# The last pair's attention weights scaled on VectorE, and gate/value products of 256 more tokens placed in the attention stage

## The chip, the cores and the metric

The kernel runs on one core of one Trainium2 chip. A core has five engines with a queue of instructions each: PE (TensorE, matrix products; PEld are its weight loads), DVE (VectorE), ACT (ScalarE), POOL (GpSimd) and SP (SyncE, which here only issues DMAs). The metric is the device time of one execution in microseconds. Three timed runs of the kernel before took 1032.08, 1032.63 and 1033.08 us; the median is 1032.63 us. The profiled execution, from which all rows below come, took 1029.82 us, of which 1028.0 us are the span from the first to the last instruction.

## The reference

Attention with a compressive memory over 4 batches, 8 heads, 576 tokens and 64 dimensions, then two gated feed-forward layers over all 2304 tokens:

```
scores = q k^T / 8, causal;  a = softmax(scores);  local = a v
phi(x) = elu(x) + 1;  mem_out = (phi(q) M_prev) / (phi(q) z_prev + 1e-6)
attn   = g * mem_out + (1 - g) * local          with g = sigmoid(beta) per head
x      = attn as 2304 tokens x 512
x      = (silu(x w_gate) * (x w_val)) w_out     w_gate, w_val: 512 x 1536, w_out: 1536 x 512
out    = act(x w_in) w_out2                     w_in: 512 x 2048, w_out2: 2048 x 512
act(h) = h if h >= 1; 0 if h <= -1; (h + 1)^2 / 4 between
```

The feed-forward weights are drawn in float64 and the activations in float32, and the kernel keeps some 22 bits: each operand of a large product is split into a high and a low part of a shorter type, and each product is done as three (high x low, low x high, high x high).

## The kernel before, in words

The kernel has two parts, each a list of tasks that a small planner (`Plan`) puts in order when the program is built. A task has an engine, an estimated duration, a priority, tasks it depends on and buffers it uses (`Inst`). The planner plays the tasks through with its estimates, each engine taking the ready task of best priority, and the instructions are emitted in the order that comes out. On the chip each engine then works through its own list in order, and waits at an instruction until what it needs is done. The estimates themselves are in no instruction.

*The attention stage* (`Attention.pair`, 0 to about 254 us) has 16 groups of tasks, one for each batch and pair of heads, called pairs here. For a pair, PE transposes keys and queries, forms the scores (`s`, L643 and L677), DVE takes the row minimum of the negated, masked scores (L657, L684), ACT forms the exponentials and their sums (L664, L695), DVE inverts the sums (`scales`, L719 and L723), and nine instructions multiply the weights `a` by that inverse and by 1 - g (`scale`, L732). These nine run on POOL. PE then transposes the scaled weights (`t`, L743, L745, L766, L783), ACT and DVE copy the transposes out of PSUM into `R` (L446), and PE forms the output with the values (`av`, L808 and L815), which ACT and DVE split into two parts and SP stores to `xs` in DRAM (L844). For phi(q), POOL folds and normalizes `p` (L581, L591). The planner gives the eight PSUM banks out one at a time, so a product waits for the copy that empties its bank.

Attention leaves PE with spare time, so part of the first feed-forward layer stands in it. `early_x` loads tokens of `xs` back into four `xh` tiles (L1144), and `early_unit` forms the gate or value product of a block of 128 columns of the weights (an f block) for these tokens: 12 products on PE (L1166), a copy by ACT into one of three `gvo` buffers (L1172) and a store to `gv` in DRAM (L1176). This is done for f blocks 0 to 5, which are three pairs of f blocks, and tokens 0 to 511. The planner is given the same tasks once more for the next two groups of tokens, as ghosts: they take time and buffers in the plan, and emit nothing.

*The second part* begins with a plain stage (`plain`, L1353, about 254 to 372 us): the rest of f blocks 0 to 5. Its tokens come in six groups of 384 (`HB`), two to a `kb`. For group 1, tokens 384 to 767, tokens 384 to 511 come from `gv` (`from_gv`: loads at L1373, silu at L1378, multiplication at L1379) and the other 256 are formed by products. Each call of `plain` fills two of eight PSUM banks, which ACT (silu, L1360) and DVE (multiplication, L1361) empty. The inputs `xw` are quarters of a group, loaded at L1275: four by POOL's queue at the end of its list, the others by SP's. Then come the f blocks 6 to 11 in a scheme with seven products in place of eight (`chain`, L1402), whose weights DVE and ACT split beforehand (L893 to L951), the product with w_out (L1480), and the second layer (L1402 again, and L1534). Order on PE is fixed there; the other engines follow by due times.

Of the kernel before, what the change touches and what calls it, by code (L numbers as in the profile page):

```python
# [18 lines left out]
P = 128  # L19
# [7 lines left out]
D0 = 6  # L27
# [13 lines left out]
HB = NT // NG  # L41
HS = S // 2
HT = 512
SET_AHEAD, PARK_AHEAD, H_AHEAD, H2_AHEAD, W_AHEAD, W2_AHEAD = 40000, 60000, 20000, 20000, 12000, 7000
MASKED = -8.0e9

# [255 lines left out]
def c_pool(n):  # L302
    return 0.835 * n + 285
# [23 lines left out]
class Attention:  # L327
# [81 lines left out]
    def pair(self, b, n):  # L409
# [15 lines left out]
        def add(eng, dur, name, fn, deps=(), uses=(), port=False, form=0):  # L425
            t = pl.add(eng, dur, at_of(name), fn, deps, uses, port=port, form=form)
            t["name"] = name
            return t
# [299 lines left out]
        def scale(key, h, i, cols, name, t_r):  # L728
            def f():
                a = st["a"][key][:, 0:cols]  # L730
                o = i if h == 0 else i + 5
                nc.gpsimd.tensor_scalar(a, a, st["mn"]["r"][:, o:o + 1], self.OGP[:, n, o:o + 1], op0=ALU.mult, op1=ALU.mult)  # L732
            return add("POOL", c_pool(cols), name + ".sc", f, [t_r], [i_a[key], i_mn])

        def tr4(t_r):
            t = scale(4, 0, 0, S, "t4", t_r)
# [354 lines left out]
def tile_attention_two_moe(  # L1091
# [11 lines left out]
    half = cst.tile([P, 1], F32, name="half")  # L1103
    nc.gpsimd.memset(half, 0.5)
    xs = dram.tile([P, KT, 2, NT], F32, name="xs")
    gv = [[dram.tile([P, 2, HT], F32, name=f"gv{i}_{j}") for j in range(2)] for i in range(D0 // 2)]
    hs = [[dram.tile([P, 2, HB], F32, name=f"hs{i}_{g}") for g in range(NG)] for i in range(F1 // 2)]
    h2s = [[dram.tile([P, 2, HB], F32, name=f"h2s{i}_{g}") for g in range(NG)] for i in range(F2 // 2)]
    wts = Weights(ctx, tc, dram)
# [5 lines left out]
    with ExitStack() as actx:  # L1115
        warm = actx.enter_context(tc.tile_pool(name="warm", bufs=1))
        plan = Plan({"PE": 4500, "POOL": 8500, "DVE": 4800}, over={"PE": 15, "ACT": 40, "DVE": 40, "POOL": 50}, lat={"DMA": 1500},
                    slow={"PE": (15500, 1.7)}, stay=STAY, turn=TURN)
        wts.pooled = True
        wts.begin(actx, plan, {"raw": 2, "wA": 3, "wS": 1}, "a", "pool")  # L1120
        still = warm.tile([P, P], F32, name="still")
        nc.vector.memset(still, 0.0)
        at = Attention(actx, tc, plan, q, k, v, M_prev, z_prev, beta, {"ident": ident}, xs)
        fpool = actx.enter_context(tc.tile_pool(name="fp", bufs=1))
        gpool = actx.enter_context(tc.tile_pool(name="gp", bufs=1))
        plan.cap("gvo", GVO), plan.cap("xh", XH)
        idle = at.ps.tile([P, HT], F32, name="idle", tag="bank7")
        for _ in range(WARM):
            nc.tensor.matmul(idle[:, 0:P], still, still, start=True, stop=True)
        for n, ((kind, f), prio) in enumerate(zip(first, EARLY)):  # L1130
            units[kind, f] = wts.early(plan, in_cols(moe_w_gate if kind == "gate" else moe_w_val, f), prio,
                                       trios[n // 3], n % 3)

        def early_x(tok, prio, deps, ghost, last):


            s, n = {"x": [None] * KT, "i": [], "t": []}, tok.stop - tok.start
            for kt in range(KT):
                i_x = plan.inst("xh")

                def f(kt=kt, i_x=i_x):
                    if not ghost:
                        s["x"][kt] = fpool.tile([P, 2, n], F32R, name="xh", tag=f"xh{i_x.slot}")
                        nc.sync.dma_start(f32(s["x"][kt]), xs[:, kt, :, tok])  # L1144

                s["i"].append(i_x)
                s["t"].append(plan.dma(prio, [n * 2.85], f, deps[kt], [i_x], last))
                last = plan.last
            return s, last

        def early_unit(f, x, prio, own, ghost):


            s = {}
            for j, kind in enumerate(("gate", "val")):
                u = units[kind, f]
                i_p, i_o = plan.inst("bank"), plan.inst("gvo")

                def prod(i, u=u, j=j, i_p=i_p):
                    if ghost:  # L1160
                        return
                    if i == 0:
                        s[j] = at.ps.tile([P, HT], F32, name="mm", tag=f"bank{i_p.slot}")
                    for kt in range(CUTS[i], CUTS[i + 1]):
                        for n, (pw, px) in enumerate(PARTS):
                            nc.tensor.matmul(s[j], u["k"](pw, kt), x["x"][kt][:, px], start=(kt == 0 and n == 0),  # L1166
                                             stop=(kt == KT - 1 and n == 2))

                def copy(j=j, i_o=i_o):
                    if not ghost:  # L1170
                        s["o", j] = gpool.tile([P, HT], F32, name="gvo", tag=f"gvo{i_o.slot}")
                        nc.scalar.copy(s["o", j], s[j])  # L1172

                def put(j=j):
                    if not ghost:
                        nc.sync.dma_start(gv[f // 2][j][:, f % 2], s["o", j])  # L1176

                t = []
                for i in range(len(CUTS) - 1):
                    cost = 3 * (CUTS[i + 1] - CUTS[i]) * (HT + 32) / 2.4  # L1180
                    t = [plan.add("PE", cost, prio - (i > 0), lambda i=i, prod=prod: prod(i),
                                  t + [*u["t"], *x["t"][CUTS[i]:CUTS[i + 1]]],
                                  [i_p, *x["i"][CUTS[i]:CUTS[i + 1]]])]
                t = plan.add("ACT", c_act(HT), prio - 1, copy, t, [i_p, i_o])
                if own:
                    t = plan.add("ACT", 50, prio - 2, put, [t], [i_o])
                    plan.add("DMA", 1.42 * HT, prio, lambda: None, [t], [i_o])
                else:
                    plan.dma(prio, [1.42 * HT], put, [t], [i_o])

        t_x, last = {}, None
        for b in range(B):
            t_x[b] = [at.pair(b, n) for n in range(NP)]
            if b < B - 1:
                tok, ghost = slice(b * HT, (b + 1) * HT), b > 0
                stored = [[t_x[e][kt] for e in range(tok.start // S, b + 1)] for kt in range(KT)]
                xh, last = early_x(tok, X_AT[b], stored, ghost, last)
                for f in range(D0):
                    early_unit(f, xh, GROUP_AT[b], b == B - 2 and f >= D0 - 2, ghost)
        with tc.manual_schedule():  # L1200
            plan.emit()

# [362 lines left out]


    for i in range(D0 // 2):
        t = flat("h")
        kept = [from_gv(i, HT - HB, HB, t, 15000)]
        ends = kept + [plain(f, qs[0], 1, slice(HT - HB, HB), t, []) for f in (2 * i, 2 * i + 1)]  # L1570
        t_hs[i, 1] = store(t, hs[i][1], ends)
    for r in range(2):
        qs[0][r, 0] = quarter(0, r, 0, 8000)
# [105 lines left out]
```

## Time and profile before

| | |
|---|---|
| median of three timed runs | 1032.63 us |
| profiled execution | 1029.82 us |
| its span | 1028.0 us |
| busy: PE, PEld, DVE, ACT, POOL | 98%, 88%, 69%, 56%, 21% |
| chain that ended last, by engine | PE 94%, POOL 3%, DMA 1%, DVE 1%, issue 1% |
| mean granted PE clock | 0.994 of full speed |

A group of the profile is one line of the kernel on one engine, written with what it writes and reads (`mm<-xw`). PE's matrix products overlap, so the time per product is the busy time of a group divided by its count, and not the mean duration of one. The busy share of PE is nearly full everywhere but for one of the forty slices of the page, the one from about 231 to 257 us, where it is 6 tenths. [...]

### The profile page before, as it was taken

The page shows a single profiled execution, that of the slowest core. Times are in us where ns is not written, and L with a number is a line of the kernel's source. Part 1 is how long each engine was busy: PE and PEld are TensorE (multiplying, and loading weights), DVE is VectorE, ACT ScalarE, POOL GpSimd, SP SyncE. Part 2 cuts the span into 40 slices and gives each one's busy share as a digit, 9 for nine tenths or more (in the row PEclk, how much of TensorE's full clock was granted, in tenths as well). Part 3 has the DMA queues.
Part 4 walks back from the last instruction along what each step waited for, and adds up shares of the span by engine and source line. Part 5 has one row for each costly group of instructions (what it writes and reads, how often), then busy time and mean ns, then how long its engine had stood idle before and what let it go on. Part 6 is the DMA issues. An engine that isn't in the chain of part 4 may idle for free.

```text
span 1028.0 us, 16598 instructions
## 1 busy us (share of the span) xinstructions
PE 1004.1 (98%) x5892; PEld 907.8 (88%) x5892; DVE 705.9 (69%) x1483; ACT 576.5 (56%) x1247; POOL 219.9 (21%) x309
## 2 busy tenths in 40 slices
PE   6999999996999999999999999999999999999998
PEld 5667777775999999999999999999999988888886
DVE  5888888874697777777858988866765346455451
ACT  5987898864333254536344444454444558566561
POOL 7899889994000000000000000000000000000000
PEclk9999999998999999999999999999999999999999
DMA  7786654324975551524986575145443596324320
GB/s 173 179 228 192 170 166 132 107 90 167 353 263 183 181 172 59 164 99 154 376 319 230 179 252 195 52 159 184 159 164 134 193 369 231 120 79 150 129 102 31
DMA packets 142883, 180.93 MB, mean 176 GB/s; under 512 B 70160, under 2 KB 99856, under 8 KB 142800
## 3 DMA queue, kind: packets, MB, share of 16 engines
q1 hardware_dynamic: 140702, 176.42, 52.0%
q0 software_dynamic: 768, 3.15, 0.9%
q8 instruction: 47, 0.77, 0.3%
q10 hardware_dynamic: 1330, 0.30, 0.1%
q14 instruction: 36, 0.29, 0.1%
HBM read 114.82 MB, written 65.01 MB: 175 GB/s over the span
## 4 chain that ended last, share of the span: by engine, by line
PE 94%; POOL 3%; DMA 1%; DVE 1%; issue 1%; SPq 0%; POOLq 0%; DVEq 0%
PE mm L1402 30%; PE mm L1534 19%; PE mm L1480 15%; PE mm L1353 11%; PE av L815 4%; PE mm L1166 3%; PE s L643 3%; PE t L766 2%; PE av L808 2%; POOL a L732 1%; PE s L677 1%; PE t L783 1%; PE tq L539 1%; PE tp L597 1%; PE tk L528 1%; PE t L743 1%
## 5 line engine op out<-in xcount | busy, mean ns | idle before, releaser
L1402 PE MATMUL mm<-xw 128*128 128x384 f32 x1512 | 269.8, 335 | 0.5 <-DVE xw L951 0.5
L1402 PEld LDWEIGHTS mm<-xw 128*128 128x128 f32 x1512 | 262.7, 188 | 0.9 <-DVE xw L951 0.8
L1534 PE MATMUL mm<-xw 128*128 128x512 f32 x864 | 196.2, 390 | 0.0
L1534 PEld LDWEIGHTS mm<-xw 128*128 128x128 f32 x864 | 162.3, 188 | 33.5
L1480 PE MATMUL mm<-xw 128*128 128x384 f32 x864 | 150.1, 334 | 0.0
L1480 PEld LDWEIGHTS mm<-xw 128*128 128x128 f32 x864 | 149.8, 188 | 0.0
L1353 PE MATMUL mm<-xw 128*128 128x384 f32 (+1 forms) x720 | 117.4, 324 | 0.0
L1353 PEld LDWEIGHTS mm<-xw 128*128 128x128 f32 x720 | 117.1, 189 | 0.2 <-issue 0.2
L732 POOL TENSOR_SCALAR a<-a,r,OGP 128x256 f32<-128x256 f32 (+4 forms) x144 | 96.1, 679 | 4.8 <-ACT a L664 3.2
L664 ACT ACTIVATE a<-a,mn 128x256 f32<-128x256 f32 (+3 forms) x128 | 71.0, 565 | 9.3 <-DVE mn L657 9.1
L1523 DVE SCALAR_TENSOR_TENSOR t<-r,t 128x768 f32<-128x768 f32 x48 | 46.0, 958 | 39.2 <-ACT t L1522 37.6
L1297 DVE TENSOR_TENSOR xw<-t,xw 128x768 fp32r<-128x768 f32 x48 | 46.0, 957 | 37.0 <-ACT xw L1294 37.0
L1294 ACT CAST xw<-t 128x768 fp32r<-128x768 f32 x48 | 40.1, 835 | 40.6 <-DVE t L1523 40.6
L657 DVE CUSTOM_DVE_ANT_0 a<-s,mask 128x512 f32<-128x512 f32 (+3 forms) x128 | 55.1, 485 | 4.9 <-PE s L643 4.5
L888 ACT ACTIVATE wA<-raw 128x512 f32<-128x512 f32 x68 | 45.6, 677 | 21.3 <-DMA raw<-in_moe_w_out_dram 15.7
L1424 ACT COPY mm<-mm 128x384 f32<-128x384 f32 x42 | 19.5, 465 | 57.5 <-PE mm L1402 57.5
L815 PEld LDWEIGHTS av<-R,vn 128*64 128x64 f32 x448 | 32.2, 137 | 21.3
L1402 PE MATMUL mm<-xw,wh 128*128 128x384 f32 x252 | 50.4, 334 | 0.0
L1520 ACT ACTIVATE t<-r,half 128x768 f32<-128x768 f32 x48 | 44.9, 936 | 8.9 <-DMA r<-h2s 8.0
L1294 ACT CAST xw<-h 128x768 fp32r<-128x768 f32 x36 | 29.7, 836 | 34.5 <-DMA h<-hs 21.2
L815 PE MATMUL av<-R,vn 128*64 128x320 f32 (+4 forms) x448 | 48.7, 357 | 0.0
L899 DVE SCALAR_TENSOR_TENSOR wA<-raw,wA 128x512 uint32<-128x512 uint32 x68 | 48.3, 716 | 0.3
(142 smaller groups left out, 1528.8 us busy)
## 6 DMA issues: line engine op xcount, KB each, us to landing
h2s<-r SPq DMA_DIRECT2D x48, 384.0 KB, 2.5
r<-h2s SPq DMA_DIRECT2D x48, 384.0 KB, 3.8
raw<-in_moe_w_out_dram SPq DMA_DIRECT2D x28, 512.0 KB, 6.3
park<-pk SPq DMA_DIRECT2D x28, 512.0 KB, 2.9
hs<-h SPq DMA_DIRECT2D x36, 384.0 KB, 4.7
h<-hs SPq DMA_DIRECT2D x36, 384.0 KB, 5.0
xw<-park SPq DMA_DIRECT2D x24, 512.0 KB, 7.9
xs<-x SPq DMA_DIRECT2D x16, 576.0 KB, 4.3
```

The source lines that it names most:

```text
L657: nc.vector.tensor_tensor_reduce(a, st[f"s{h}{tag}"][:, at_[c]:at_[c] + kl[c]], self.mask0[:, 512 - kl[c]:512], -0.125, 3.0e38, ALU.add, A ...
L664: nc.scalar.activation(a, a, AF.Exp, bias=mn[:, o:o + 1], scale=-1.0, accum_out=sm[:, o, 0:1])
L732: nc.gpsimd.tensor_scalar(a, a, st["mn"]["r"][:, o:o + 1], self.OGP[:, n, o:o + 1], op0=ALU.mult, op1=ALU.mult)
L815: nc.tensor.matmul(o[rg][halves[h], c0:c1], st["vn"][:, kc, h], r, start=False, stop=i == len(terms[rg]) - 1, tile_position=(0, h * 64), s ...
L899: nc.vector.scalar_tensor_tensor(s["F"], words(s["raw"])[:, :, 1], 0xC0000000, s["F"], op0=ALU.bitwise_and, op1=ALU.bitwise_or)
L1294: nc.scalar.copy(s["x"][:, :, 0], t())
L1297: nc.vector.tensor_sub(s["x"][:, :, 1], t(), f32(s["x"][:, :, 0]))
L1353: nc.tensor.matmul(o[:, 0:n], u["k"](pw, kt), qs[kt // 2, c]["at"](px, kt % 2)[:, span], start=(kt == 0 and i == 0), stop=(kt == KT - 1 an ...
L1402: nc.tensor.matmul(o, S["k"](k, pw, j), x[k]["at"](px, j), start=begin and not (i or j), stop=j == 1 and i == 2, skip_group_check=True)
L1480: nc.tensor.matmul(o, u["k"](pw, m), h["at"](px, j), start=(i == 0 and j == 0 and n == 0), stop=(i == F1 // 2 - 1 and j == 1 and n == 2), ...
L1523: x1 = add_dve(2 * HB, lambda raw=raw, t=t: nc.vector.scalar_tensor_tensor(t["get"](), raw["get"](), 1.0, t["get"](), op0=ALU.max, op1=ALU ...
L1534: nc.tensor.matmul(o, h["at"](px, j)[:, m * P:(m + 1) * P], u["w"][:, pw], start=(i == 0 and j == 0 and n == 0), stop=(i == F2 // 2 - 1 an ...
```

## The change

Two things are changed. For the last of the 16 pairs, the nine scales of L732 are issued on DVE, and the planner counts them there; the other fifteen stay on POOL. And the f blocks 0 and 1 get tokens 512 to 767 in the attention stage too (`GV` says up to which token each pair of f blocks is done there): `early_x` now loads these 256 tokens into `xh`, and four units form their products with 256 columns. Their results go to `gv`, and in the plain stage group 1 of these two blocks is read from `gv` whole, 384 columns, without products. For the other blocks, and for the last group of tokens, the tasks stay ghosts; the sizes that the planner is told for ghosts follow the slices of tokens, so they are smaller.

```diff
--- before.py
+++ after.py
@@ -41,6 +41,7 @@
 HB = NT // NG
 HS = S // 2
 HT = 512
+GV = (768, 512, 512)
 SET_AHEAD, PARK_AHEAD, H_AHEAD, H2_AHEAD, W_AHEAD, W2_AHEAD = 40000, 60000, 20000, 20000, 12000, 7000
 MASKED = -8.0e9
 
@@ -729,8 +730,11 @@
             def f():
                 a = st["a"][key][:, 0:cols]
                 o = i if h == 0 else i + 5
-                nc.gpsimd.tensor_scalar(a, a, st["mn"]["r"][:, o:o + 1], self.OGP[:, n, o:o + 1], op0=ALU.mult, op1=ALU.mult)
-            return add("POOL", c_pool(cols), name + ".sc", f, [t_r], [i_a[key], i_mn])
+                eng.tensor_scalar(a, a, st["mn"]["r"][:, o:o + 1], self.OGP[:, n, o:o + 1], op0=ALU.mult, op1=ALU.mult)
+
+            eng = nc.vector if num == B * NP - 1 else nc.gpsimd
+            return add(*(("DVE", c_dve(cols)) if num == B * NP - 1 else ("POOL", c_pool(cols))), name + ".sc", f, [t_r],
+                       [i_a[key], i_mn])
 
         def tr4(t_r):
             t = scale(4, 0, 0, S, "t4", t_r)
@@ -1103,7 +1107,7 @@
     half = cst.tile([P, 1], F32, name="half")
     nc.gpsimd.memset(half, 0.5)
     xs = dram.tile([P, KT, 2, NT], F32, name="xs")
-    gv = [[dram.tile([P, 2, HT], F32, name=f"gv{i}_{j}") for j in range(2)] for i in range(D0 // 2)]
+    gv = [[dram.tile([P, 2, GV[i]], F32, name=f"gv{i}_{j}") for j in range(2)] for i in range(D0 // 2)]
     hs = [[dram.tile([P, 2, HB], F32, name=f"hs{i}_{g}") for g in range(NG)] for i in range(F1 // 2)]
     h2s = [[dram.tile([P, 2, HB], F32, name=f"h2s{i}_{g}") for g in range(NG)] for i in range(F2 // 2)]
     wts = Weights(ctx, tc, dram)
@@ -1148,10 +1152,10 @@
                 last = plan.last
             return s, last
 
-        def early_unit(f, x, prio, own, ghost):
-
-
-            s = {}
+        def early_unit(f, x, tok, prio, own, ghost):
+
+
+            s, size = {}, tok.stop - tok.start
             for j, kind in enumerate(("gate", "val")):
                 u = units[kind, f]
                 i_p, i_o = plan.inst("bank"), plan.inst("gvo")
@@ -1163,17 +1167,17 @@
                         s[j] = at.ps.tile([P, HT], F32, name="mm", tag=f"bank{i_p.slot}")
                     for kt in range(CUTS[i], CUTS[i + 1]):
                         for n, (pw, px) in enumerate(PARTS):
-                            nc.tensor.matmul(s[j], u["k"](pw, kt), x["x"][kt][:, px], start=(kt == 0 and n == 0),
+                            nc.tensor.matmul(s[j][:, 0:size], u["k"](pw, kt), x["x"][kt][:, px], start=(kt == 0 and n == 0),
                                              stop=(kt == KT - 1 and n == 2))
 
                 def copy(j=j, i_o=i_o):
                     if not ghost:
-                        s["o", j] = gpool.tile([P, HT], F32, name="gvo", tag=f"gvo{i_o.slot}")
-                        nc.scalar.copy(s["o", j], s[j])
+                        s["o", j] = gpool.tile([P, size], F32, name="gvo", tag=f"gvo{i_o.slot}")
+                        nc.scalar.copy(s["o", j], s[j][:, 0:size])
 
                 def put(j=j):
                     if not ghost:
-                        nc.sync.dma_start(gv[f // 2][j][:, f % 2], s["o", j])
+                        nc.sync.dma_start(gv[f // 2][j][:, f % 2, tok], s["o", j])
 
                 t = []
                 for i in range(len(CUTS) - 1):
@@ -1192,11 +1196,11 @@
         for b in range(B):
             t_x[b] = [at.pair(b, n) for n in range(NP)]
             if b < B - 1:
-                tok, ghost = slice(b * HT, (b + 1) * HT), b > 0
+                tok = slice(b * HT, min((b + 1) * HT, GV[0]))
                 stored = [[t_x[e][kt] for e in range(tok.start // S, b + 1)] for kt in range(KT)]
-                xh, last = early_x(tok, X_AT[b], stored, ghost, last)
+                xh, last = early_x(tok, X_AT[b], stored, b == 2, last)
                 for f in range(D0):
-                    early_unit(f, xh, GROUP_AT[b], b == B - 2 and f >= D0 - 2, ghost)
+                    early_unit(f, xh, tok, GROUP_AT[b], b == B - 2 and f >= D0 - 2, b * HT >= GV[f // 2])
         with tc.manual_schedule():
             plan.emit()
 
@@ -1565,9 +1569,10 @@
 
 
     for i in range(D0 // 2):
-        t = flat("h")
-        kept = [from_gv(i, HT - HB, HB, t, 15000)]
-        ends = kept + [plain(f, qs[0], 1, slice(HT - HB, HB), t, []) for f in (2 * i, 2 * i + 1)]
+        t, n = flat("h"), GV[i] - HB
+        ends = [from_gv(i, n, HB, t, 15000)]
+        if n < HB:
+            ends += [plain(f, qs[0], 1, slice(n, HB), t, []) for f in (2 * i, 2 * i + 1)]
         t_hs[i, 1] = store(t, hs[i][1], ends)
     for r in range(2):
         qs[0][r, 0] = quarter(0, r, 0, 8000)
```

The two kernels have the same order on every engine up to about 226 us. Three places follow.

On PE, at the end of the attention stage (`t` transposes of weights, `a_3369` and `a_3339` those of the pair before the last, `a_3574` and `a_3552` of the last), before:

```order
L766 MATMUL t_3548<-ident,a_3369 128x128 x3
L766 MATMUL t_3555<-ident,a_3339 128x128 x4
L743 MATMUL t_3563<-ident,a_0_237 128x128 x4
L745 MATMUL t_3568<-ident,a_0_237 128x128
L766 MATMUL t_3610<-ident,a_3574 128x128 x3
L766 MATMUL t_3616<-ident,a_3552 128x128 x3
```

and in the changed kernel, where the lines after 1100 stand four higher, L1170 is L1166 and the last pair's weights are `a_3577` and `a_3560`:

```order
L770 MATMUL t_3556<-ident,a_3369 128x128 x3
L1170 MATMUL mm<-xh,xw 128x256 x48
L770 MATMUL t_3665<-ident,a_3577 128x128 x3
L770 MATMUL t_3671<-ident,a_3560 128x128 x3
L770 MATMUL t_3677<-ident,a_3339 128x128 x4
L770 MATMUL t_3682<-ident,a_3553 128x128 x4
L770 MATMUL t_3688<-ident,a_3543 128x128 x4
```

The 48 products stand behind the first three transposes; four transposes of the pair before the last and that pair's `t` of L743 and L745 now come behind them, the latter as the last but one group ahead of the output's products.

On DVE, from the sums of the last pair on (`r` the inverse sums, `OGP` the factors 1 - g), before:

```order
L719 TENSOR_REDUCE r<-sum_225 128x5
L723 RECIPROCAL r<-r 128x5
L719 TENSOR_REDUCE r<-sum_225 128x4
L723 RECIPROCAL r<-r 128x4
L446 COPY R_3625<-t_3616 128x3x128
```

and in the changed kernel:

```order
L724 RECIPROCAL r<-r 128x5
L733 TENSOR_SCALAR a_3571<-a_3571,r,OGP 128x256
L733 TENSOR_SCALAR a_3573<-a_3573,r,OGP 128x128
L733 TENSOR_SCALAR a_3543<-a_3543,r,OGP 128x512
L733 TENSOR_SCALAR a_3560<-a_3560,r,OGP 128x384
L720 TENSOR_REDUCE r<-sum_225 128x4
L733 TENSOR_SCALAR a_1_238<-a_1_238,r,OGP 128x576
L724 RECIPROCAL r<-r 128x4
L733 TENSOR_SCALAR a_3581<-a_3581,r,OGP 128x256
L733 TENSOR_SCALAR a_3590<-a_3590,r,OGP 128x128
L733 TENSOR_SCALAR a_3553<-a_3553,r,OGP 128x512
L733 TENSOR_SCALAR a_3577<-a_3577,r,OGP 128x384
```

The nine scales stand between the sums and the copies of transposes, four of them ahead of the second head's sum; the copies to `R` follow them, among them one that stood ahead of the sums.

On SP, from the store of the third pair from the end on, before:

```order
L844 DMA xs<-x 128x2x576
L1176 DMA gv_0_70<-gvo 128x512
L844 DMA xs<-x 128x2x576
L1373 DMA h<-gv_0_68 128x2x128
L1373 DMA v<-gv_1_69 128x2x128
L844 DMA xs<-x 128x2x576
```

and in the changed kernel:

```order
L848 DMA xs<-x 128x2x576
L1148 DMA xh<-xs 128x2x256 x3
L1180 DMA gv_0_70<-gvo 128x512
L1148 DMA xh<-xs 128x2x256
L1180 DMA gv_0_68<-gvo 128x256
L1180 DMA gv_1_69<-gvo 128x256
L1180 DMA gv_0_68<-gvo 128x256
L1180 DMA gv_1_69<-gvo 128x256
L848 DMA xs<-x 128x2x576
L1377 DMA h<-gv_0_68 128x2x384
L848 DMA xs<-x 128x2x576
L1377 DMA v<-gv_1_69 128x2x384
```

Four loads of `xh` and four stores of `gv` with 256 columns are new, all ahead of the last two pairs' stores, and the first load of `h` now stands ahead of the last pair's store. On POOL the nine scales are gone from the end of the list, so its four loads of `xw` follow the last pair's product `p` (L591) directly.

## Rows read from the trace of the kernel before

**Rows 1.** chain that ended last, by time: start us, us, what

```profile
240.27 1.19 POOL a L732 x2
...
371.78 86.33 PE mm L1402 x498
...
459.16 0.61 DVE xw L951
```

**Rows 2.** timeline of PE: start us, us, instruction, operands, count [idle before <-releaser]

```profile
232.65 0.98 PE L766 MATMUL t<-ident,a 128*128 128x128 f32 x7
...
242.16 3.05 PE L766 MATMUL t<-ident,a 128*128 128x128 f32 x14 [7.98 <-POOL a L732]
...
246.88 0.76 PE L808 MATMUL av<-P,MZ 128*64 128x320 f32 x4
...
254.39 7.82 PE L1353 MATMUL mm<-xw 128*128 128x256 f32 x63
```

**Rows 3.** timeline of POOL at the end of the attention stage

```profile
236.25 1.15 POOL L591 TENSOR_TENSOR p<-p,nrm 128x576 f32<-128x576 f32 x1 [2.83 <-DVE nrm L587]
237.38 5.52 POOL L732 TENSOR_SCALAR a<-a,r,OGP 128x256 f32<-128x256 f32 x9
242.85 3.20 POOL L1275 DMA_DIRECT2D xw<-xs  x4
```

**Rows 4.** windows: us, busy PE PEld DVE ACT POOL, PEclk, DMA share, GB/s

```profile
231.00:234.00 3.00, 3.00 (x26) 2.29 (x24) 2.54 (x11) 1.81 (x6) 2.26 (x4) 1.00 0.01 3
...
237.00:240.00 3.00, 0.00 (x0) 0.00 (x0) 0.34 (x2) 0.78 (x4) 3.00 (x6) 0.67 0.00 0
...
244.00:245.00 1.00, 1.00 (x7) 1.00 (x6) 0.70 (x2) 0.00 (x0) 1.00 (x2) 0.56 0.73 83
245.00:246.00 1.00, 1.00 (x11) 1.00 (x10) 0.94 (x2) 0.43 (x1) 1.00 (x2) 1.00 0.68 207
```

**Rows 5.** waits from 254 us on: engine line <- releaser: us, times, longest

```profile
PEld mm L1402 <- DVE xw L951: 0.8, 1, 0.8
...
DVE h L1361 <- PE mm L1353: 14.4, 15, 2.5
```

**Rows 6.** groups by line and shape: count, busy us, mean ns, idle

```profile
L893 DVE TENSOR_SCALAR wA<-wA 128x512 f32<-128x512 f32 x56 | 23.6, 422 | 21.0 <-ACT wA L888 20.9
...
L951 DVE TENSOR_TENSOR pk<-wA,pk 128x512 fp32r<-128x512 f32 x28 | 19.2, 686 | 3.5 <-ACT pk L949 3.5
...
L1353 PE MATMUL mm<-xw 128*128 128x256 f32 x144 | 17.5, 284 | 0.0
```

**Rows 7.** timeline of SP, whose instructions issue DMAs

```profile
229.49 0.33 SPq L1176 DMA_DIRECT2D gv<-gvo  x1
...
258.71 1.15 SPq L1275 DMA_DIRECT2D xw<-xs  x2
```

**Rows 8.** DMA issues: tiles, queue, count, KB each, median us to landing

```profile
xw<-xs SPq DMA_DIRECT2D x8, 768.0 KB, 12.2
...
gv<-gvo SPq DMA_DIRECT2D x12, 256.0 KB, 6.6
...
v<-gv SPq DMA_DIRECT2D x3, 128.0 KB, 4.6
```

**Rows 9.** timeline of all engines inside the gap

```profile
234.59 0.85 ACT L446 COPY R<-t 128x256 f32<-128x256 f32 x4
234.75 0.69 DVE L446 COPY R<-t 128x512 f32<-128x512 f32 x1
...
236.55 0.19 DVE L723 RECIPROCAL r<-r 128x5 f32<-128x5 f32 x1
...
237.58 0.20 ACT L664 ACTIVATION_READ_ACCUMULATOR a<-a,mn 128x1 f32 x1
```

**Rows 10.** line 893 up to 250 us: duration ns min/median/max, first and last start

```profile
L893 DVE TENSOR_SCALAR wA<-wA x12: 397/427/873, 9.3 to 208.1; 128x512 f32<-128x512 f32 x12
```

**Rows 11.** timeline of DVE ahead of the stage at L1402

```profile
369.12 0.42 DVE L951 TENSOR_TENSOR xw<-wC,xw 128x256 fp32r<-128x256 f32 x1
```

## The prediction

> **What bounds the kernel now.** I read the page first: PE is busy for 98% of the span and carries 94% of the chain that ended last, so a change pays where PE stands still, or where it leaves PE less to do. The forty slices show one dip, in slice 10, about 231 to 257 us. There the chain in order of time [rows 1] leaves PE for L732 on POOL, and then runs on PE without a break from 371.78 to 458.11 us. The PE timeline [rows 2] shows the dip as one gap: seven transposes at 232.65, then fourteen at 242.16 behind an idle time of 7.98 us, from 234.18 on, that POOL ended. The POOL timeline [rows 3] says what it did meanwhile: the product p of the last pair to 237.40, then nine scales in a row until 242.90. [...] So this place costs 7.98 us of idle time and half of 2.7 us, 1.35: 9.3 us in all. Behind 254.39 PE waits for nothing longer than 0.8 us [rows 5].
>
> **The change, part by part.** *Products that leave the second stage.* 144 products of 256 columns at L1353 took 17.5 us of PE [rows 6], 0.1215 us each. 48 of them go (two f blocks, gate and value, 12 each): 48 x 0.1215 = 5.83 us. They stood in a stretch where PE waits for nobody, so all of it comes off, if what follows is ready 5.83 us earlier (below).
>
> *The same 48 products in the attention stage.* PE issues them behind three of the seven transposes, at 232.65 + 3/7 of 0.82 (to the next line's start) = 233.0, for 5.83 us, to 238.8. That is inside the gap, so their cost is nothing as long as the gap would have been there; what covers them is the wait for the last pair's scaled weights. Nine transposes that stood ahead of the gap (1.2 us) move behind them; they filled PE before and fill it after, so they cancel.
>
> *Their inputs.* Four loads of xh, 256 KB each, stand on SP's queue around the store of 229.49 [rows 7]. The buffers come free as the last 512-column products read them; the last of the four is issued behind that store, at about 229.9. A store of the same 256 KB issued at 229.49 left no more than a share of 0.01 of the DMA engines busy after 231 [rows 4], so under 2 us; by that the last load lands at 232. PE first reads that tile at its 16th product, 233.0 + 15 x 0.12 = 234.8: free. By the other end, 6.6 us, the median of such stores in busier stretches [rows 8], it lands at 236.5 and costs 1.7 us. I take nothing, the quiet store being the nearer row.
>
> *The nine scales, from POOL to DVE.* First, when they can start. DVE had a copy of 0.69 us at 234.75 ahead of the sums, ACT four copies of 0.85 us at 234.59 ahead of the last exponentials [rows 9]; both feed from the nine moved transposes and now stand later. So the reciprocal that ended at 236.74 ends near 235.9, and the exponentials of the other head, which ended at 237.78, end at 236.9. The scales cover 576 + 2 x 1280 = 3136 columns. No scale of this form runs on DVE in this trace. The nearest row is an operation of one input by constants, 422 ns for 512 columns [rows 6]: 3136/512 x 0.422 = 2.6 us. The far end is an operation on two inputs, 686 ns [rows 6]: 4.2 us. With the second sum and reciprocal between them (0.35) DVE ends at 235.9 + 2.95 = 238.9, or at 240.5. The first transpose behind the products waits for the ninth scale, since that is the tile it reads. At 2.6 us it is ready as the products end (238.8); at 4.2 us PE loses 1.6. I take the former: it too has one tensor input.
>
> *What is late next.* With POOL out of the way PE goes from products to transposes without its idle time, and the clock has no reason to fall. The step is worth 7.98 + 1.35 - 5.83 = 3.5 us at the first product of the attention output, which moves from 246.88 [rows 2] to 243.4. The rest to the second stage, 254.39 - 246.88 = 7.5 us, is unchanged: first product at 250.9.
>
> *The added copies and stores.* ACT copies four products out behind its exponentials, from 236.9 on. There are three gvo buffers, so the fourth copy waits until the first store has landed; behind it on ACT stand eleven copies of transposes, and the fourth group of transposes on PE needs its bank, at about 240.1. First store issued at 237.4: by the quiet store, under 2 us, it lands by 239.4 and costs nothing; by the median of 6.6 us [rows 8] it lands at 244.0 and PE loses 4.3. POOL's four loads of 768 KB now start about 5.5 us earlier (242.85 before [rows 3]) and will be on the same DMA engines, so I put 0.4 us here.
>
> *The second stage's inputs.* PE wants them 3.5 to 9.3 us earlier. The four POOL loads follow p directly, at 237 rather than 242.85, and are first read at 250.9: earlier by 5.8 for 3.5. SP's own xw loads start at 258.71 [rows 7], behind the stores of the last two pairs, so they follow PE and move by some 3. The first pair, landing by 258.71 + 12.2 [rows 8] = 271 even if nothing moved, is wanted at 250.9 + 96 x 0.1215 + 48 x 0.173 (products of 384 columns, 498 in 86.33 us [rows 1]) = 270.9. Free. The value load of the first f pair grows from 128 to 384 columns; DVE needs it early but PE only once eight banks are full.
>
> *Weights of the next stage.* The one wait behind 254, 0.8 us at 459 [rows 1, 5], is for DVE splitting a set of weights. Nothing ahead of that split on its engine waits for a PE product later than the 8th before its use; in the changed order it is the 20th. Whether the wait goes cannot be read from an order; I count half, 0.4.
>
> **Sum.** 5.83 + 3.50 - 0.4 + 0.4 = 9.3 us less. Against the profiled execution, 1029.8 us with a span of 1028.0, that is 1020.5. That execution is 2.8 us below the median of the three timed runs, 1032.63; the same 9.3 us from the median gives 1023.3.
>
> **The rivals.** *A, DVE and POOL in each other's way.* An operation of one input took DVE 397 to 873 ns while POOL worked [rows 10], against 422 where it did not [rows 6]. POOL's p, 1.15 us, now starts near 235.7 and overlaps the first scale. If that scale waits for p's end, all of DVE's chain slips 0.9 us, and PE with it: 1024.2. For it: the 873; against it: the median there is 427. [...]
>
> *B, the tail waits for the store or for slow scales.* The prices are above: up to 4.3 for the store's landing, 1.6 for scales at the two-input rate. For it: the median of 6.6 and POOL's loads in the same microseconds; against it: the quiet store. With 3 us lost: 1026.3.
>
> *C, DVE becomes the bound of the stage that follows.* The last split of the first set of weights ended at 369.54 [rows 11], 2.2 us ahead of the stage that reads it at 371.78 [rows 1]. If DVE keeps its times while PE comes 9.3 us earlier, PE waits about 7.1: 1030.4. Against it: DVE itself waits 14.4 us for PE in that stretch [rows 5], and the loads of the set are tied to PE's progress.
>
> *D, slower than before.* DVE's queue now has the multiplication by the larger value load ahead of the third f block's. Its load is issued behind the last pair's store, near 252.5; with the 4.6 us of the smaller one [rows 8] it lands at 257. PE goes on into eight free banks, four blocks of 2.9 us, until 262.6. Each microsecond that the load lands later than that is one lost, and from 271.9 on the change is slower than before; at 275 the time is 1035.8. Nothing in the trace is so late: the longest median is 12.2.
>
> **How the numbers follow.** Forecast 0.58, A 0.20, B 0.14, C 0.05, D 0.03. The range: upward B with its full prices together would be 5.9 us, 1029.2, and I cut it at 1028.0; downward a whole 0.8 at 459 and no loss at the store give 1022.5, and another 1 us for what the new order may save gives 1021.5. 1021.5 to 1028.0 leaves out C, D, the end of B and a little below. What tells a change from none here is about 0.2%, 2.1 us. Faster by more: forecast, A, B and half of C (it gives 2.2), 0.945; within: 0.025; slower: D, 0.03.
>
> **What would show it.** Right: 48 L1170 products of 256 columns on PE from about 233.0, no half clock between 230 and 260, the attention output's products at 243.4, the first L1357 at 250.9 and its line at 672 products. The nine scales on DVE in 2.6 us, ended by 239. A wait of the fourth gvo copy on ACT, or of PE's fourth group of transposes, would be B; a first scale of 1 us or more A; a wait of PE before the first L1406 C; banks held for a value load D. The forecast is wrong if PE's gap is only shorter instead of gone, or if a wait of several microseconds appears behind 254.

## The result, and the profile after

The changed kernel took 1023.32 us (median of four runs, 1021.81 to 1024.29), beside 1032.36 for the kernel before in the same series: a ratio of 0.9913, 95% interval 0.9896 to 0.993. In a second series (experiment *after_again*) the medians were 1023.70 and 1031.02, a ratio of 0.9928, 0.9915 to 0.994. The forecast was 1023.3. The number came out; one step behind it did not.

PE's timeline at the end of the attention stage, changed kernel (columns as in [rows 2]):

```profile
234.66 0.55 PE L770 MATMUL t<-ident,a 128*128 128x128 f32 x3
234.96 6.03 PE L1170 MATMUL mm<-xh,xw 128*128 128x256 f32 x48
242.79 2.19 PE L770 MATMUL t<-ident,a 128*128 128x128 f32 x18 [1.80 <-DVE a L733]
...
247.20 0.76 PE L812 MATMUL av<-P,MZ 128*64 128x320 f32 x4
...
254.77 7.45 PE L1357 MATMUL mm<-xw 128*128 128x256 f32 x60
```

The 48 products fill the gap as forecast, but behind them PE still stands still for 1.80 us, and DVE, not POOL, now ends that. The transposes that started at 232.65 before [rows 2] start at 234.66 here, though up to there both kernels have the same order. So this execution was 2.0 us late before the change had begun; the reason is in PE's clock, in windows around 20 us (columns as in [rows 4]). First the kernel before, then the changed one:

```profile
20.00:23.00 3.00, 2.57 (x12) 2.02 (x11) 1.10 (x3) 2.04 (x6) 3.00 (x5) 0.50 0.59 134
23.00:26.00 3.00, 3.00 (x23) 2.56 (x23) 2.33 (x7) 1.46 (x7) 2.29 (x4) 1.00 0.77 219
```

```profile
20.00:23.00 3.00, 2.18 (x11) 1.90 (x10) 1.08 (x3) 1.58 (x5) 3.00 (x5) 0.53 0.64 145
23.00:26.00 3.00, 3.00 (x12) 2.45 (x11) 1.14 (x3) 1.30 (x4) 2.02 (x3) 0.50 0.79 188
```

In both PE runs at half clock (0.50) from about 20 us; before, full clock was back by 23, here not by 26. PE's first transposes of weights start at 18.93 in both, and a product of scores behind them 1.97 us apart, the kernel before first:

```profile
25.68 1.77 PE L643 MATMUL s<-K,S 64*128 64x512 f32 x8
```

```profile
27.65 1.77 PE L644 MATMUL s<-K,S 64*128 64x512 f32 x8
```

Such a difference moves everything behind it, here by 2 us. The runs scatter by as much (1021.8 to 1024.3), but *split_busy* below shows that the early clock isn't the only cause of that. So the two traces are compared by stage, each from the same instruction on:

| stage | before | changed | less | forecast |
|---|---|---|---|---|
| transposes of the pair before the last (232.65, 234.66) to the first product of the second stage (254.39, 254.77) | 21.74 | 20.11 | 1.63 | 3.5 |
| from there to the end of the span (1028.0, 1022.5) | 773.61 | 767.73 | 5.88 | 5.83 |
| sum | | | 7.5 | 9.3 |

7.5 us is a ratio of 0.9927, inside both measured intervals; 9.3 us, 0.991, is inside the first alone. In the trace of *after_again* the first stage took 20.11 us again and the second 768.8, which makes 6.5 us less in all: the second stage varies by 1 us. Within it, PE's plain stage alone, as the chain that ended last has it, got 5.71 us shorter, the kernel before first:

```profile
254.46 117.32 PE mm L1353 x720
```

```profile
254.78 111.61 PE mm L1357 x672
```

The clock did not fall at the gap any more, where it had read 0.67 and 0.56 [rows 4]:

```profile
237.00:240.00 3.00, 3.00 (x27) 3.00 (x26) 2.77 (x9) 2.58 (x12) 2.34 (x3) 1.00 0.00 0
240.00:242.00 2.00, 0.99 (x9) 0.78 (x7) 1.96 (x7) 0.74 (x2) 2.00 (x3) 1.00 0.82 174
```

What DVE and POOL did meanwhile, where POOL's timeline had nine scales in 5.52 us [rows 3]; DVE first:

```profile
238.03 2.29 DVE L733 TENSOR_SCALAR a<-a,r,OGP 128x256 f32<-128x256 f32 x4
240.24 0.15 DVE L720 TENSOR_REDUCE r<-sum 128x4 f32<-128x8 f32 x1
240.31 0.57 DVE L733 TENSOR_SCALAR a<-a,r,OGP 128x576 f32<-128x576 f32 x1
...
241.00 1.74 DVE L733 TENSOR_SCALAR a<-a,r,OGP 128x256 f32<-128x256 f32 x4
```

```profile
237.66 1.15 POOL L592 TENSOR_TENSOR p<-p,nrm 128x576 f32<-128x576 f32 x1 [2.23 <-DVE nrm L588]
238.75 3.35 POOL L1279 DMA_DIRECT2D xw<-xs  x4
```

The scales run from 238.03 to 242.74: 4.7 us with the second sum and reciprocal between them, against a forecast of 2.95. By the three rows the scales alone are 4.6, against 2.6. The first, of 256 columns, took 0.93 beside POOL's p, its twin without p 0.48. ACT's fourth `gvo` copy waited for the first store as the prediction said it would, without harm, since it ended 1.1 us ahead of the transposes:

```profile
241.33 0.37 ACT L1176 COPY gvo<-mm 128x256 f32<-128x256 f32 x1 [0.60 <-DMA gv<-gvo]
```

In the second stage the 144 products of 256 columns [rows 6] are 96:

```profile
L1357 PE MATMUL mm<-xw 128*128 128x256 f32 x96 | 11.8, 284 | 0.0
```

PE's wait for split weights at 459 us [rows 1, 5] is gone, and a new one stands where PE begins the product with w_out: "PE mm L1484 <- DMA xw<-park". The 0.8 us of [rows 5] are the wait of the weight loads (PEld), for which the new wait is 0.7. PE's products themselves waited 0.5 us before, and 0.3 here or 0.9 in *after_again*.

### The profile page after: what moved, and what is told of

The parts are those of the page before. It is cut to its first block, busy times and chain, and to the rows that moved or that the text cites. A ratio compares the mean times of both kernels' runs of the same rounds, so it can differ in the third digit from the quotient of the medians.

```text
span 1022.5 us, 16609 instructions
## 1 busy us (share of the span) xinstructions
PE 1005.3 (98%) x5892; PEld 908.2 (89%) x5892; DVE 711.5 (70%) x1490; ACT 577.8 (57%) x1249; POOL 214.5 (21%) x300
## 4 chain that ended last, share of the span: by engine, by line
PE 93%; DMA 2%; POOL 2%; ACT 1%; DVE 1%; issue 0%; SPq 0%; ACTq 0%; DVEq 0%; POOLq 0%
PE mm L1406 30%; PE mm L1538 19%; PE mm L1484 13%; PE mm L1357 11%; PE av L819 4%; PE mm L1170 4%; PE s L644 3%; PE t L770 2%; PE av L812 2%; PE s L678 1%; POOL a L733 1%; DMA hs<-h 1%; PE t L787 1%; DMA xw<-park 1%; PE tp L598 1%; PE tq L540 1%
## 5 line engine op out<-in xcount | busy, mean ns | idle before, releaser
L1406 PE MATMUL mm<-xw 128*128 128x384 f32 x1512 | 269.5, 334 | 0.0
L1406 PEld LDWEIGHTS mm<-xw 128*128 128x128 f32 x1512 | 262.8, 188 | 0.1
L1484 PE MATMUL mm<-xw 128*128 128x384 f32 x864 | 150.4, 335 | 0.3 <-DMA xw<-park 0.3
L1484 PEld LDWEIGHTS mm<-xw 128*128 128x128 f32 x864 | 149.8, 188 | 0.7 <-DMA xw<-park 0.7
L1357 PE MATMUL mm<-xw 128*128 128x384 f32 (+1 forms) x672 | 111.6, 327 | 0.0
L733 POOL TENSOR_SCALAR a<-a,r,OGP 128x256 f32<-128x256 f32 (+4 forms) x135 | 90.7, 683 | 5.2 <-ACT a L665 3.4
L1406 PE MATMUL mm<-xw,wh 128*128 128x384 f32 x252 | 50.5, 334 | 0.0
L897 DVE TENSOR_SCALAR wA<-wA 128x512 f32<-128x512 f32 x68 | 29.6, 436 | 25.5 <-ACT wA L892 24.1
```

The lines of the kernel that those rows point to most:

```text
L733: eng.tensor_scalar(a, a, st["mn"]["r"][:, o:o + 1], self.OGP[:, n, o:o + 1], op0=ALU.mult, op1=ALU.mult)
L1357: nc.tensor.matmul(o[:, 0:n], u["k"](pw, kt), qs[kt // 2, c]["at"](px, kt % 2)[:, span], start=(kt == 0 and i == 0), stop=(kt == KT - 1 an ...
L1406: nc.tensor.matmul(o, S["k"](k, pw, j), x[k]["at"](px, j), start=begin and not (i or j), stop=j == 1 and i == 2, skip_group_check=True)
L1484: nc.tensor.matmul(o, u["k"](pw, m), h["at"](px, j), start=(i == 0 and j == 0 and n == 0), stop=(i == F1 // 2 - 1 and j == 1 and n == 2), ...
```

## The experiments

**The two halves of the change alone.** *scales_only* is the kernel before with the nine scales on DVE (the edit at L732 of the diff above); *products_only* is the changed kernel with that edit undone.

> Only the first half of the change: the last pair's nine scales on DVE, no extra products. The gap of PE before the transposes stays and begins where it did (234.2 us in the trace of before). Theory S (a scale of this form runs on DVE at the 4.7 us that the changed kernel's trace shows from the first to the end of the ninth, so the first transposes of the last pair start near 236.7 + 4.7 = 241.4 in place of 242.2): 0.7 us less than before, the half clock stays, about 1031.7 us. Theory F (the forecast's 2.6 us for nine scales was right and POOL's work beside them cost the rest): up to 2.6 us less, 1029.8. Rival (most of the 9 us comes from this half): 3 us less or more.

Measured: 1030.40 us to 1030.99, ratio 0.9994 (0.9985 to 1.0003): no gain that can be told. PE's wait was shorter, but the second stage began later, 22.40 us behind the transposes at 232.34, where before it was 21.74:

```profile
241.07 3.25 PE L769 MATMUL t<-ident,a 128*128 128x128 f32 x14 [7.20 <-DVE a L732]
...
254.74 3.50 PE L1356 MATMUL mm<-xw 128*128 128x256 f32 x27
```

```profile
243.00:244.00 1.00, 1.00 (x7) 1.00 (x6) 0.70 (x2) 0.00 (x0) 0.00 (x0) 0.50 1.02 384
244.00:245.00 1.00, 1.00 (x7) 1.00 (x6) 0.84 (x2) 0.01 (x1) 0.00 (x0) 0.50 0.96 370
245.00:246.00 1.00, 1.00 (x6) 0.96 (x5) 0.20 (x2) 0.47 (x1) 0.00 (x0) 0.50 1.02 384
```

Theory S had the wait right (0.78 us less for 0.7), and in this execution the clock took it back: here it was still at half at 246 and full again at 246.7, in the trace of before at 244.9. The clock had fallen at 236.5, 2.6 us after PE's last product, where the kernel before took 3.8 (from 234.18 [rows 2] to 238.0, by the 0.67 of [rows 4]). The interval of the times holds both S's 0.7 us and no gain. Theory F and the rival fall.

> Only the other half: the 48 products in the attention stage, the nine scales on POOL. The products run in PE's gap, then PE waits for POOL's ninth scale. Theory S: 5.83 us of products leave the second stage, PE's idle time shrinks from 8.0 to about 3.5 us (products end 2 to 4 us ahead of the scales on POOL), and PE stands still too briefly for its clock to fall, so 5.8 + 1.3 less and a little for sums that start earlier: 7.1 to 7.6 us less than before, some 1025 us, 1.7 above the changed kernel. Rival (the clock falls all the same): 5.8 less, 1026.5. Rival (the scales on DVE give nothing): 1023.3 as the changed kernel.

Measured: 1025.53 us to 1030.99, ratio 0.9941 (0.9929 to 0.9954), 6.1 us less by the interval's middle. PE waited less than expected, since p and with it POOL's scales started earlier, and its clock stayed full:

```profile
232.55 6.31 PE L1167 MATMUL mm<-xh,xw 128*128 128x256 f32 x48
241.17 2.18 PE L767 MATMUL t<-ident,a 128*128 128x128 f32 x18 [2.30 <-POOL a L733]
```

The interval, 4.7 to 7.3 us less, holds the lower end of theory S and the rival's 5.8, but the clock speaks against the rival: it read 1.00 from 234 to 246 us. By stage this trace is 6.8 us shorter than before: 20.89 us for 21.74, and 767.66 for 773.61. So the products carry nearly all of the change. The scales on DVE shorten the wait from 2.30 to 1.80 and the first stage by 0.78 us, from 20.89 to 20.11; with both halves PE is still idle there.

**What a scale costs on DVE.** Both kernels below are the changed one with instructions added behind its end.

```
for c in (128, 256, 384, 512):
    3 x nc.vector.tensor_scalar(a[:, 0:c], a[:, 0:c], r, g, ...)        # two columns of a tile
    3 x nc.vector.tensor_scalar(a[:, 0:c], a[:, 0:c], 0.5, 0.75, ...)   # two constants
3 x tensor_scalar by one column, 3 x tensor_mul, 512 columns
```

> The changed kernel with DVE instructions added behind its end, first alone and then again while POOL works through 20 multiplications of 576 columns: scales by two columns of a tile, 128 to 512 columns, the same by two constants, by one column, and a product of two tiles. Theory P (the form costs it: factors read from a tile take longer than constants, with or without POOL): 512 columns by two tile columns take about 0.70 us alone, by constants 0.42, and POOL beside them changes neither by much. Theory Q (POOL costs it): both take 0.42 alone, and both 0.7 or more with POOL at work. From the changed kernel's trace the first of the nine, 256 columns beside POOL's p, took 0.93 and its twin without it 0.48, so a part of Q is expected in either case.

POOL's multiplications wait for nothing that DVE does here, so they ran beside the first set, and the second set ran alone. Alone (DVE by line and shape: count, busy us, mean ns, idle; L1666 two columns, L1670 one, L1668 constants):

```profile
L1666 DVE TENSOR_SCALAR xw<-xw 128x512 f32<-128x512 f32 x3 | 1.6, 546 | 0.1
L1670 DVE TENSOR_SCALAR xw<-xw 128x512 f32<-128x512 f32 x3 | 1.5, 486 | 0.1
...
L1668 DVE TENSOR_SCALAR xw<-xw 128x512 f32<-128x512 f32 x3 | 1.3, 427 | 0.1
...
L1666 DVE TENSOR_SCALAR xw<-xw 128x128 f32<-128x128 f32 x3 | 1.0, 346 | 0.1
...
L1668 DVE TENSOR_SCALAR xw<-xw 128x128 f32<-128x128 f32 x3 | 0.7, 227 | 0.1
```

Beside POOL (DVE, then POOL):

```profile
L1666 DVE TENSOR_SCALAR xw<-xw 128x384 f32<-128x384 f32 x3 | 4.4, 1459 | 0.1
L1668 DVE TENSOR_SCALAR xw<-xw 128x384 f32<-128x384 f32 x3 | 4.3, 1441 | 0.1
L1668 DVE TENSOR_SCALAR xw<-xw 128x128 f32<-128x128 f32 x3 | 4.3, 1439 | 0.1
```

```profile
L1663 POOL TENSOR_TENSOR xw<-xw 128x576 f32<-128x576 f32 x20 | 28.0, 1402 | 782.3 <-DVE xw L1659 780.8
```

Both theories hold a part. From 128 to 512 columns the time grows by 0.200 us with either kind of factor, 0.52 ns a column. What differs is the part that every instruction pays whatever its size: 0.16 us with constants, 0.28 with two columns of a tile, 0.06 for each column. The forecast, by scaling 422 ns per 512 columns, counted the smaller of the two 6.1 times (3136/512) for nine instructions. And beside POOL's multiplication each DVE instruction, of 128 or of 384 columns, takes the 1.4 to 1.5 us of one POOL instruction: the two go in turns. Once POOL's stream runs, each DVE instruction of 128 to 384 columns starts 0.04 to 0.17 us behind the start of a POOL one and ends behind its end, by 0.08 us with 128 columns and by 0.21 with 384.

> The changed kernel with the nine scales, in the sizes and the order that DVE has them in, run three times more behind its end: alone, beside five DMAs issued by POOL, and beside two multiplications on POOL. From the single instructions measured (128 columns 0.346, 256 0.412, 384 0.479, 512 0.546, all waiting for the one before): nine that don't wait for each other take some 3.5 us alone. Theory D (issuing DMAs on POOL holds DVE up): 4.2 us or more beside the DMAs. Theory M (only POOL's arithmetic does): 3.5 beside the DMAs, and about 1.4 more for each of the two multiplications that it meets.

```
nine = [256, 128, 512, 384, 576, 256, 128, 512, 384]   # columns, each on its own part of a tile
scaled(); five nc.gpsimd.dma_start(...); scaled(); two nc.gpsimd.tensor_mul(...); scaled()
```

```profile
1026.47 3.43 DVE L1663 TENSOR_SCALAR xw<-xw 128x256 f32<-128x256 f32 x9
...
1033.55 3.48 DVE L1663 TENSOR_SCALAR xw<-xw 128x256 f32<-128x256 f32 x9
...
1045.19 3.24 DVE L1663 TENSOR_SCALAR xw<-xw 128x256 f32<-128x256 f32 x9
```

The nine alone take 3.43 us, as expected: 1.63 for 3136 columns and 0.20 for each instruction, less than the 0.28 of one that waits for the one before. The third set met no multiplication, since these had ended at 1041.5, and so is a second measurement alone, 3.24 behind a memset as the second set is. The set beside the DMAs, which were issued until 1035.8, took 3.48: 0.24 more, so nearer to M. In the changed kernel the nine took 4.6, 1.2 more than alone: 0.5 of it is the first scale beside p (0.93 for 0.41), and 0.4 the two of 512 columns, 0.80 and 0.70 for 0.54, which met the issue of POOL's larger loads. That these loads are the cause of the latter is argued from the times alone, and scales of 128, 384 and 576 columns met the same issue without loss (0.33, 0.46 and 0.57 us). The rest stays open.

**Is the wait of 1.8 us all that is left?** *head0_first* changes the planner's priorities for the last pair, so that PE transposes the first head's weights ahead of the second's:

```diff
+        LAST = {"t02": -53900, "t03": -53800, "t01": -53700, "t12": 40000, "t13": 41000, "t11": 42000} if num == B * NP - 1 else {}
-        at_of = lambda name: num * 100 + (FIRST_ORDER if ... else ORDER)[name]
+        at_of = lambda name: num * 100 + LAST.get(name, (FIRST_ORDER if ... else ORDER)[name])
```

> The changed kernel with one thing moved: for the last pair, PE transposes the weights of the first head (whose scales end on DVE 2.4 us before the ninth) ahead of those of the second. Theory S (the 1.8 us that PE still stands still in the changed kernel are the wait for the ninth scale and nothing else): the wait goes, no other takes its place, 1.8 us less than the changed kernel, 1021.5. Rival (the end of the attention stage then waits for DVE's copies, which stand behind the scales, or for a bank held by the fourth gvo copy): 0 to 0.5 us less.

Measured: 1021.81 us to 1030.99, ratio 0.9914 (0.9901 to 0.9928). The wait for the scales is gone, and a shorter one has come, for a copy that stands behind the scales on DVE:

```profile
241.91 0.63 PE L599 MATMUL tp<-ident,p 128*128 128x128 f32 x4 [0.57 <-DVE R L448]
```

From the transposes to the second stage it is 19.03 us, 1.08 less than in the changed kernel: between theory and rival. Theory S was wrong that no other wait takes its place; the rival named the copies, and its price was too high. For a comparison on one chip it ran again beside the changed kernel:

> The changed kernel once more, for a comparison on one chip with the kernel below that transposes the first head first and with the split one: 9 us less than before (ratio 0.991).

> The kernel that transposes the first head first, beside the changed kernel on one chip. Its trace had 0.57 us of waiting left of 1.80 and reached the second stage's first product 1.1 us earlier, counted from the scores of the last pair. Theory: 1.1 us less than the changed kernel (ratio 0.990 to before's 0.991). Rival (what it saves comes back as the wait for parked weights, 0.7 us in its trace): 0.3 us less, not to be told from none.

Measured: 1023.70 us (0.9928, 0.9915 to 0.994) and 1022.07 us (0.9906, 0.9891 to 0.9921), to 1031.02. The ratios differ by 0.0022, twice what was expected, and the intervals overlap, so the times alone don't settle it. The traces repeat the 1.1 us: from the transposes to the second stage 19.05 us beside 20.11, and the changed kernel's wait was 1.81 us again.

*split* shares the nine scales out, four for POOL and five for DVE:

```diff
-            eng = nc.vector if num == B * NP - 1 else nc.gpsimd
+            eng = nc.vector if num == B * NP - 1 and (h or key == 4) else nc.gpsimd
...
```

The line below it, which tells the planner, has the same condition.

> The changed kernel with the last pair's nine scales shared out: the first head's four on POOL, the other five on DVE. Theory L (DVE and POOL hold each other up operation by operation, as in the lock step of 1.47 us seen when both worked): DVE's last scale ends some 4.7 us after the first sums as before, PE's wait stays near 1.8 us, no gain. Theory I (the two work side by side): POOL's four take 2.4 us behind p, DVE's five end with the second sums plus 1.7 us, some 1.4 us earlier than in the changed kernel, PE's wait shrinks to 0.4, and the time by 1.4 us.

Measured: 1021.46 us, ratio 0.9906 (0.9892 to 0.9919). PE, DVE and POOL:

```profile
239.76 2.38 PE L770 MATMUL t<-ident,a 128*128 128x128 f32 x18 [0.15 <-DVE a L733]
```

```profile
236.38 1.10 DVE L733 TENSOR_SCALAR a<-a,r,OGP 128x576 f32<-128x576 f32 x1
...
237.84 1.86 DVE L733 TENSOR_SCALAR a<-a,r,OGP 128x256 f32<-128x256 f32 x4
```

```profile
237.14 3.09 POOL L733 TENSOR_SCALAR a<-a,r,OGP 128x256 f32<-128x256 f32 x4
```

Theory I is nearer: the wait shrinks to 0.15, and from the transposes to the second stage it is 18.92 us, 1.19 less than in the changed kernel. The two do hold each other up (1.10 for the 0.57 of 576 columns, 3.09 for some 2.4: the same four took POOL 0.555, 0.450, 0.769 and 0.662 in *products_only*, with DVE quiet), but not in turns throughout.

**Two steps further.** *more_products* is *split* with `GV = (768, 768, 512)`.

> The split kernel with 48 products more taken into the attention stage (f blocks 2 and 3, tokens 512 to 767), in the same place. PE's gap there is 0.15 us in the split kernel. Theory G (a moved product pays only what gap it fills): the output of the attention stage comes 5.7 us later, the second stage has 5.8 us less to do, and the time stays at 1021.5, or a little above if the stores in the tail get in the way. Rival (each moved product pays its 0.12 us): 5.8 less, 1015.7.

Measured: 1050.88 us, ratio 1.0185 (1.0168 to 1.0202), 19.7 us slower than before. Neither theory gives that time. The chain that ended last and PE's waits:

```profile
240.98 8.26 DMA gv<-gvo
...
249.34 0.37 ACT gvo L1176
```

```profile
PE mm L1484 <- DMA xw<-park: 17.4, 4, 9.6
PE t L770 <- ACT R L447: 4.6, 1, 4.6
```

The eighth copy waits for a buffer, whose store lands 8.26 us after the copy that it follows, beside POOL's loads (DMA share 0.95 to 1.05 from 242 to 250 us): rival B's mechanism, and PE's 4.6 us are near the 4.3 that the prediction gave it. From the transposes to the second stage it is 30.32 us, 11.4 more than in *split*: 5.5 for the products, as theory G says, 4.6 for this wait, and PE at half clock behind it (0.50 from 251 to 253 us). The larger part of the loss comes later: the parked weights of the product with w_out are no longer there in time, 17.4 us. Whether the order of the queues, the transfers or the smaller amount of PE work ahead is at fault was not tried.

*split_busy* tests the early half clock: 16 products that nobody reads, where PE waits for the first pair's first scale.

```diff
+            if num == 0 and cs[0] == 1:
+                i_d = bank()
+                def idle():
+                    x = psum("idle", i_d)
+                    for _ in range(16):
+                        nc.tensor.matmul(x[:, 0:P], self.ident, self.ident, start=True, stop=True)
+                pl.add("PE", 10, -90000, idle, [t_q], [i_d], form=1)
```

> The split kernel with 16 products of 128 columns added, that nobody reads, where PE waits 3.9 us for the first pair's first scale (15.0 to 18.9 us). In every trace so far PE's clock is at half from about 19 or 20 us on, and comes back at 22 in one execution and at 27 in another, which moves all that follows by up to 2 us. Theory W (that wait causes the fall): no half clock between 18 and 28 us, 1.3 to 3 us less than the split kernel, about 1019.5, and less scatter among the runs. Rival (the fall has another cause, or POOL and not PE sets the pace there): no gain, 1021.5.

PE's timeline, where each of these products stands as two instructions, and the windows of above:

```profile
14.83 3.84 PE L657 MATMUL idle<-ident 128*128 128x128 f32 x32
```

```profile
20.00:23.00 3.00, 2.18 (x18) 1.99 (x18) 1.45 (x6) 1.96 (x5) 3.00 (x5) 1.00 0.56 126
23.00:26.00 3.00, 3.00 (x21) 1.95 (x19) 3.00 (x7) 2.43 (x9) 3.00 (x5) 1.00 0.82 214
```

The clock stays at 1.00, where in *split* it read 0.55 and 0.88 in the same windows: PE's idle time was the cause. Measured: 1020.36 us to 1031.14, ratio 0.9888 (0.987 to 0.9905), the lowest of all; over *split* that is 0.0018, with overlapping intervals, so its gain is likely and not shown. The runs still scatter by 2 us (1019.36 to 1021.39), three of them with a mean clock of 1.000: that part of the theory fails, and what else scatters the runs stays open.

## Why the prediction was right, and where it was not

- *The products that leave the second stage*: right. 5.83 us forecast, 5.71 measured for the plain stage and 5.88 for the whole second part, net of the small waits that went and came there.
- *The same products in the gap*: right. They ran without a wait for their inputs, 6.03 us by the timeline.
- *The nine scales*: the step that failed is "3136/512 x 0.422 = 2.6 us". That PE's transposes wait for DVE's ninth scale was right, the size was not: nine instructions pay a fixed part nine times and read their factors from a tile (3.4 us alone), and in the kernel they took 4.6, with 0.5 shown to come from POOL's p beside the first. The upper end of 4.2 us was nearer, its price of 1.6 us for PE close to the 1.80 measured. By the prediction's own mark, "The forecast is wrong if PE's gap is only shorter instead of gone", this part was wrong.
- *The clock*: right. PE stands still for 1.8 us in place of 8.0, and its clock reads 1.00 throughout. No run shows the 1.35 us of the sum by itself: it is an estimate, half of the 2.7 us from 242.16 to the return at 244.9 (by the 0.56 of [rows 4]). From 242.16 on fourteen transposes took 3.05 us [rows 2], where the changed kernel has eighteen in 2.19.
- *From the attention output to the second stage*: 7.57 us for 7.5, so the 0.4 set aside for colliding transfers was not needed.
- *The wait at 459 us*: 0.4 was put down as the mean of gone and not gone, from the 0.8 us of the weight loads; PE's products had waited 0.5. It went, and 0.3 to 0.9 came back at L1484, so it gave 0.2 us in one execution and took 0.4 in the other.
- *Rivals*: A's hold-up is there, at 0.5 us (0.93 for 0.41) for its 0.9. B came by its slow scales, and not by the store. C and D did not show: no wait ahead of the first L1406, none for a value load.
- *The number*: 9.3 us were forecast and 9.0 and 7.3 measured in two series, 7.5 and 6.5 by the traces. That the first median met the forecast to 0.1 us is luck, since the runs scatter by 2 us and PE lost 1.8 us that the sum had put at nothing; that error is inside the range because the range had held B's price.

## What to carry to other kernels

Work moved into PE's idle time paid in full here as long as there was idle time left (5.88 us for 48 products); one dose more turned 9.6 us of gain (*split*) into 20 of loss, only part of which was traced to its cause. A short DVE scale's time was a fixed part plus 0.52 ns a column, so take both parts from two rows of the same form, and count the fixed part once for each instruction (0.28 us for one that waits for the one before, 0.20 in a string that doesn't). Before two traces are compared, measure each from the last instruction that they have in common: here that took 2 us of early clock out of the answer.

## What the runs showed of the hardware

- A DVE scale by columns of a tile takes 0.06 us more for each such factor than one by a constant (0.546, 0.486 and 0.427 us for 512 columns); for two factors it is the same 0.12 us at 128 columns (0.346 and 0.227).
- DVE scales beside a stream of POOL multiplications take 1.44 to 1.46 us, whether they have 128 or 384 columns (0.23 to 0.48 alone); POOL's four scales beside DVE's took 3.09 us for 2.4.
- PE's clock fell to half just behind its early wait of 3.9 to 4.4 us, when PE was working again (the wait ended at 18.93, the clock fell at 19.6 in the kernel before and at 20.2 in the changed one; 17.96 and 18.0 in *scales_only*), and stayed at full where 16 unread products filled the wait. How long it then stays at half differs between executions of the same work: until 21.4 (*scales_only*), 23 or 27 us at the start, and until 244.9 (the kernel before) or 246.7 (*scales_only*) at the end of the attention stage.
